# Scatter parts two attention units apart, and joined 512-column second products in the 256-token slots

## The chip, the cores and the metric

The kernel runs on one core of a Trainium2 chip. The metric is the device time of one execution in microseconds (us), as the median of several runs. Engines are called PE (matrix products), PEld (the loading of weights for them), DVE (vector), ACT (activation), POOL (GpSimd) and SP (which only issues DMAs here).

## What is computed

An attention without softmax is followed by a mixture of eight experts, each token going to one expert. All numbers are float32, and the kernel keeps that accuracy by splitting operands in a high and a low part.

```python
# B, S, D = 8, 2496, 256; d_qk = 64; E, F = 8, 1024
scores = matmul(z, z.T) / S
x = u * matmul(maximum(scores, 0) ** 2, v)          # per batch
logits = x @ w_gate
e = argmax(logits); gate = softmax(logits)[e]
eom = sigmoid(x @ w_output_gate)
h = maximum(x @ w1[e], 0)                            # F = 1024
out = gate * eom[e] * (h @ w2[e])
```

## The kernel before

**Attention.** For each of 8 batches there are 5 chunks of queries (the first has 448 columns, the others 512), and for each chunk 10 key pairs. One (batch, chunk, pair) is a unit; there are 400, in the order of the list `units`. A unit has `scores` or `take` (the attention matrix of the pair, made by PE, ACT and DVE two units ahead, `LOOK`) and `weigh` (line 394), its products with v: 10 or 12 matmuls into the two PSUM banks of the chunk.

**The tail of a chunk.** When a chunk is done, a `Tail` (line 414) takes its result through gating, logits, choice of expert and position, and at last a scatter of the token rows to the table `xs` in DRAM. Each unit that follows calls `advance` (line 598) of every living tail once, behind its `weigh`. So a step of the tail falls on one unit, and `TAIL` is the number of the last step that does something; a tail is kept until its step count reaches it. Steps 0 to 9 fall on the ten units of the next chunk, and from step 10 on the tail runs beside its successor. The scatter itself has four parts: `scatter_part` (line 577) issues one small ACT instruction that turns row numbers to integers (`idx`, line 581) and then 3 or 4 indirect DMAs on POOL (line 585), each for 128 segments of token rows. Their data lie in `xr` (line 469), which has two buffers, so a tail's buffer is written again by the transpose of the tail after the next (line 470). SP and POOL run in the order in which the program is written, and so do PE, ACT and DVE.

**Experts.** The tokens of an expert stand together in `xs`, and slots read them: 27 + 3 slots of 512 tokens, 7 of 288 to 480, and 8 of 256 that always run. Ten more of 256 run only under two `tc.If` when the counts of tokens want them. A slot's `up` (line 988) makes one bank of hidden values (two of the eight blocks f in a 256-token slot, four banks in all), `down` (line 1017) the second product of that bank. `run` (line 1266) lets `down` follow three `up`s later (`BEHIND`), and the last slot of a run has its second products in one piece in `whole` (line 1035), first for 128 tokens (part 0), then for the other 128 (part 1).

**The second product of a 256-token slot.** `term` (line 1046) makes for a block f and a part three matmuls of 256 columns: hidden high times weight low, hidden low times weight high, hidden high times weight high, all added into the first 256 columns of a PSUM bank. The hidden values are the stationary operand here and the weights the moving one:

```python
for k, (hx, ww) in enumerate(((hh, 1), (hl, 0), (hh, 0))):
    w = wb[4 + f // 2][:, ww]
    y, st, mv = self.o[part][:, :D], hx[:, at + part * P : ...], w[:, ds_ : ds_ + D]
```

`end_rows` (line 1068) scales the bank by the gate and moves it to `y` with one ACT instruction for each part; `finish` (line 1123) then writes the rows to the output with indirect DMAs on POOL. The wider slots (`columns`, line 1076) use the other orientation and aren't touched.

**Between the two.** The list `later` spreads the last two tails' steps over the first slots (lines 1252 to 1262).

Of the kernel before, what the change touches and what calls it, by code (L numbers as in the profile page):

```python
# [11 lines left out]
AF = mybir.ActivationFunctionType  # L12
ALU = mybir.AluOpType
# [4 lines left out]
P = 128  # L18
B, S, D, DQ = 8, 2496, 256, 64
# [5 lines left out]
T = 256  # L25
# [34 lines left out]

REST = S - (NCH - 1) * CH - 2 * P

TAIL = 15

N_HELD = 2

# [10 lines left out]
def attention_moe(ctx, tc, zt, zq_in, ut, v, wg, w12, out):  # L77
    nc = tc.nc
# [25 lines left out]
        out=sums[0:32].rearrange("p (a m) -> p a m", a=4),  # L104
        in_=ones[0:32].rearrange("p (a m) -> p a m", a=4),
# [308 lines left out]
    class Tail:  # L414
# [183 lines left out]
        def advance(self):  # L598
            k = self.step
            self.step += 1  # L600
            (
                self.gate,
                lambda: (self.split(0), self.split(1)),
                self.rows,
                self.logits,
                self.turn,
                self.choose,
                self.pick,
                self.factor,
                lambda: (self.finish(), self.place()),  # L610
                self.scatter,
                lambda: None,
                lambda: self.scatter_part(0),
                lambda: self.scatter_part(1),
                lambda: self.scatter_part(2),
                lambda: self.scatter_part(3),
                lambda: None,
            )[min(k, TAIL)]()


    def t1(name, shape, dt=F32, tag=None):
        return pool.tile([1] + shape, dt, name=name, tag=tag or name)
# [247 lines left out]
    def pads():  # L870

        pad = pool.tile([P, ROW], F32, name="pad", tag="lt")
        nc.gpsimd.memset(pad, 0.0)
        nc.gpsimd.memset(pad.bitcast(I32)[:, SEG - 1 : SEG], NOTOK)
        ends = t1("ends", [E], I32)
        nc.vector.tensor_copy(out=ends, in_=carry[0][0:1])
        yield
        for e in range(E + 1):
            if e < E:
                at = nc.sync.value_load(ends[0:1, e : e + 1], min_val=e * CAP, max_val=e * CAP + N)  # L880
                seg = xs_rows[bass.ds(at, TW), :]
            else:
                seg = xs_rows[E * CAP : E * CAP + TW, :]
            it = nc.sync.dma_start(
                out=seg.rearrange("(p q) d -> p q d", q=4), in_=pad.unsqueeze(1).to_broadcast([P, 4, ROW])
            )
            tc.add_to_no_dep_group(last_scatters, it.ins)
            yield
# [3 lines left out]
    class Slot:  # L892
# [142 lines left out]
        def whole(self):  # L1035

            self.o = [ps_o.tile([P, CH], F32, name="o") for _ in range(2)]
            self.begin_rows()
            for part in range(2):
                for f in range(8):  # L1040
                    self.term(f, part)
                self.end_rows(part)
            if not self.held:
                self.finish()

        def term(self, f, part):

            wb, n = self.w, self.n
            bank, at = self.hidden(f)
            hh, hl = self.h[bank]  # L1050
            ds_ = (f % 2) * D
            for k, (hx, ww) in enumerate(((hh, 1), (hl, 0), (hh, 0))):
                w = wb[4 + f // 2][:, ww]
                if n == T:
                    y, st, mv = self.o[part][:, :D], hx[:, at + part * P : at + (part + 1) * P], w[:, ds_ : ds_ + D]
                else:
                    y, st, mv = self.o[part][:, :n], w[:, ds_ + part * P : ds_ + (part + 1) * P], hx[:, :n]
                nc.tensor.matmul(  # L1058
                    out=y, lhsT=st, rhs=mv, start=f == 0 and k == 0, stop=f == 7 and k == 2
                )  # L1060
# [4 lines left out]
            else:  # L1065
                self.y = pool.tile([P, 4, D], F32, name="y", tag="xr", bufs=2)

        def end_rows(self, q):
            nc.scalar.activation(
                out=self.y[:, q].rearrange("p (a k s) -> p k a s", a=4, k=2),  # L1070
                in_=self.o[q][:, :D].rearrange("p (k a s) -> p k a s", a=4, k=2),
                func=AF.Copy,
                scale=self.m[:, q, 0:1],
            )

        def columns(self):
            n = self.n
# [102 lines left out]
    def prepare(k):  # L1180
        while to_load and to_load[0][0] - to_load[0][1] <= k:
            to_load.pop(0)[2].load()
        while to_split and to_split[0][0] <= k:
            to_split.pop(0)[2].split()

    attn = {}
    tail = nxt = o = None
    tails = []
# [23 lines left out]
    for k, (b, c, jp) in enumerate(units):  # L1212
# [16 lines left out]
        if b == B - 1:  # L1229
# [4 lines left out]
            at = (c, pos)  # L1234
# [11 lines left out]
        if pos == NPAIR - 1:  # L1246
            tail = nxt
            tails = [it for it in tails if it.step < TAIL] + [tail]
        prepare(k)
# [1 line left out]

    idle = lambda: None
    later = [idle] * (4 * 12)
    for k in (0, 2, 6, 10, 14):
        later[k] = tails[0].advance
    for k in (*range(1, 22, 2), 22, 29, 32, 35):
        later[k] = tail.advance
    more, fill = other_tables(), pads()
    for _ in range(29):
        later += [idle, lambda: next(more, None)]  # L1260
# [73 lines left out]
    with tc.If(used > N_MAIN + 1):  # L1334
        part = slots[last + 1 :]
# [63 lines left out]
```

## Time and profile before

| | us |
|---|---|
| runs: median (lowest, highest) | 2200.44 (2196.61, 2205.82), 3 runs |
| the profiled execution's own time | 2191.03 |
| its span in the trace | 2189.2 |
| PE busy | 2163.7 (99%) |
| PEld busy | 1828.4 (84%) |
| DVE busy | 1752.4 (80%) |
| ACT busy | 1452.0 (66%) |
| POOL busy | 940.2 (43%) |

How to read it: "busy" is the time in which an engine had an instruction in work. Matmuls overlap each other, and the end of one is modelled, so the share of PE says that it hardly ever starved and not how fast it went; that is read from the starts of successive matmuls. The granted PE clock is 0.99 to 1.00 of full speed in all 40 slices of the page. Attention lasts to about 1310 us, the 256-token slots run from about 2090 us to the end.

### The profile page before, as it was taken

How to read it: one execution, taken by the hardware profiler on the slowest of the kernel's cores; microseconds unless marked ns; L12 is line 12 of the kernel's file. 1: busy time of each engine (PE TensorE's matmuls, PEld its weight loads, DVE VectorE, ACT ScalarE, POOL GpSimd, SP SyncE). 2: the span in 40 equal slices, each digit the busy share in tenths (PEclk: the TensorE clock that was granted, in tenths of full speed). 3: DMA queues.
4: the chain of work that ended last, by engine and by line, in shares of the span. 5: the costliest groups of instructions: out<-in, count | busy, mean ns of one | idle time of the engine just before them, and what ended most of it. 6: DMA issues, size and time to landing. Idle time of an engine off the chain costs nothing. (4 is left out here: it accounts for less than half of the span.)

```text
span 2189.2 us, 35155 instructions
## 1 busy us (share of the span) xinstructions
PE 2163.7 (99%) x10207; PEld 1828.4 (84%) x10207; DVE 1752.4 (80%) x2884; ACT 1452.0 (66%) x2494; POOL 940.2 (43%) x829
## 2 busy tenths in 40 slices
PE   9999999999999999999999999999999999999998
PEld 7888788788788788888788888888888898888998
DVE  8898898898898898898898897676666766666676
ACT  8768768768778767767768765555555555555565
POOL 1365565565565564665565574321212111121222
PEclk9999999999999999999999999999999999999999
DMA  6695795794785785784784694535566766666542
GB/s 211 210 240 169 215 242 167 215 241 167 222 235 171 222 232 166 223 234 166 217 239 163 216 266 114 150 95 154 178 188 188 217 210 200 198 187 201 184 148 79
DMA packets 467738, 423.88 MB, mean 194 GB/s; under 512 B 156077, under 2 KB 366638, under 8 KB 467536
## 3 DMA queue, kind: packets, MB, share of 16 engines
q1 hardware_dynamic: 439952, 379.97, 59.3%
q0 software_dynamic: 27584, 41.58, 5.5%
q8 instruction: 82, 1.34, 0.3%
q14 instruction: 120, 0.98, 0.1%
HBM read 292.21 MB, written 158.66 MB: 206 GB/s over the span
## 5 line engine op out<-in xcount | busy, mean ns | idle before, releaser
L585 POOL DMA_INDIRECT xs<-xr,idx x624 | 766.1, 1228 | 597.8 <-ACT idx L581 422.1
L403 PE MATMUL o<-ah,v 128*128 128x512 f32 (+1 forms) x3200 | 845.8, 387 | 9.0 <-ACT ah L277 6.9
L403 PEld LDWEIGHTS o<-ah,v 128*128 128x128 f32 x3200 | 596.1, 188 | 120.7 <-ACT ah L277 10.7
L403 PE MATMUL o<-al,v 128*128 128x512 f32 (+1 forms) x1520 | 463.8, 386 | 0.5
L1012 ACT ACTIVATE hh<-sc 128x512 fp32r<-128x512 f32 (+7 forms) x328 | 190.1, 580 | 391.1 <-PE sc L1003 348.8
L1125 POOL DMA_INDIRECT out<-y,meta x156 | 159.0, 1019 | 629.1 <-ACT y L1115 558.3
L1013 DVE SCALAR_TENSOR_TENSOR hl<-sc,hh 128x512 fp32r<-128x512 f32 (+7 forms) x328 | 218.2, 665 | 262.3 <-ACT hh L1012 248.5
L1003 PE MATMUL sc<-xh,w 128*128 128x512 f32 (+8 forms) x1440 | 399.0, 362 | 1.8 <-issue 1.8
L1058 PE MATMUL o<-hh,w 128*128 128x512 f32 (+7 forms) x1184 | 400.2, 379 | 0.0
L403 PEld LDWEIGHTS o<-al,v 128*128 128x128 f32 x1520 | 283.9, 188 | 58.6 <-DVE al L281 6.6
L281 DVE TENSOR_TENSOR al<-a,ah 128x1024 fp32r<-128x1024 f32 (+1 forms) x199 | 233.1, 1171 | 111.0 <-ACT ah L277 91.0
L1003 PEld LDWEIGHTS sc<-xh,w 128*128 128x128 f32 x1440 | 258.2, 188 | 40.6 <-issue 1.3
L272 ACT ACTIVATE a<-sc 128x512 f32<-128x512 f32 (+1 forms) x398 | 207.6, 572 | 105.9 <-PE sc L271 44.1
L1058 PEld LDWEIGHTS o<-hh,w 128*128 128x128 f32 x1184 | 221.2, 188 | 38.9
L957 DVE TENSOR_TENSOR w<-raw,w 128x512 fp32r<-128x512 f32 x368 | 246.1, 680 | 2.8 <-ACT w L956 2.2
L1058 PE MATMUL o<-hl,w 128*128 128x512 f32 (+7 forms) x592 | 224.5, 379 | 0.0
L956 ACT CAST w<-raw 128x512 fp32r<-128x512 f32 x368 | 220.1, 615 | 0.0
L385 ACT CAST ah<-z 128x1024 fp32r<-128x1024 f32 x192 | 199.5, 1047 | 20.9 <-DMA z<-td 17.3
L275 ACT ACTIVATE a<-a 128x1024 f32<-128x1024 f32 (+1 forms) x199 | 203.6, 1023 | 6.3
L1003 PE MATMUL sc<-xl,w 128*128 128x512 f32 (+8 forms) x720 | 202.3, 362 | 0.0
L389 DVE TENSOR_TENSOR al<-z,ah 128x1024 fp32r<-128x1024 f32 x160 | 194.5, 1216 | 8.3 <-ACT ah L385 3.8
L270 PE MATMUL sc<-z,hl 128*128 128x512 f32 (+1 forms) x398 | 152.8, 384 | 5.0 <-ACT a L272 4.2
(201 smaller groups left out, 2395.5 us busy)
## 6 DMA issues: line engine op xcount, KB each, us to landing
raw<-in_w SPq DMA_DIRECT2D x368, 256.0 KB
z<-td SPq DMA_DIRECT2D x647, 128.0 KB
td<-t SPq DMA_DIRECT2D x160, 512.0 KB
raw<-in_v SPq DMA_DIRECT2D x80, 256.0 KB
u<-in_ut SPq DMA_DIRECT2D x32, 512.0 KB
ym<-yd SPq DMA_DIRECT2D x126, 128.0 KB
sx<-xs SPq DMA_DIRECT2D x120, 128.0 KB
yd<-yt SPq DMA_DIRECT2D x30, 512.0 KB
```

The lines of the kernel that those rows point to most:

```text
L272: nc.scalar.activation(out=a[:, q, :w], in_=sc[:, :w], func=AF.Relu)
L275: nc.scalar.activation(out=a[:, :, :w], in_=a[:, :, :w], func=AF.Square)
L281: nc.vector.tensor_tensor(out=al[:, :, :w], in0=a[:, :, :w], in1=ah[:, :, :w].bitcast(F32), op=ALU.subtract)
L385: nc.scalar.copy(out=ah, in_=z)
L389: nc.vector.tensor_tensor(out=al, in0=z, in1=ah.bitcast(F32), op=ALU.subtract)
L403: nc.tensor.matmul(out=o[d][:, :w], lhsT=vv[:, q, d * P : (d + 1) * P], rhs=rhs, start=begins and q == 0 and k == 0, stop=ends and q == 1 ...
L585: it = nc.gpsimd.indirect_dma_start(out=xs[:, :], out_offset=bass.IndirectOffsetOnAxis(ap=idx[:, n - first : n - first + 1], axis=0), in_= ...
L956: nc.scalar.copy(out=ww[:, 0], in_=wr)
L957: nc.vector.tensor_tensor(out=ww[:, 1], in0=wr, in1=ww[:, 0].bitcast(F32), op=ALU.subtract)
L1003: nc.tensor.matmul(out=hp[:, at : at + n], lhsT=wb[2 * d + f // 4][:, ww, fs], rhs=xx[:, d, :], start=k == 0, stop=k == 5,)
L1013: nc.vector.scalar_tensor_tensor(out=lo, in0=hp[:, 0:used], scalar=0.0, in1=ho.bitcast(F32), op0=ALU.max, op1=ALU.subtract)
L1058: nc.tensor.matmul(out=y, lhsT=st, rhs=mv, start=f == 0 and k == 0, stop=f == 7 and k == 2)
```

## The change

Two separate edits. The first moves parts 1, 2 and 3 of a chunk's scatter from steps 12, 13 and 14 of the tail to 13, 15 and 17, with empty steps between, and so `TAIL` from 15 to 18. The two tails that are still living when attention ends call `scatter_part` by name from the list `later`, at the positions that they had. The second edit, in the 256-token slots, makes of three matmuls two: hidden high times the pair (weight high, weight low) as one product of 512 columns into both halves of a PSUM bank, and hidden low times weight high into the first half. `end_rows` then adds the second half, scaled, to `y` with two DVE instructions for each part. Only part 1 of `whole` keeps the three matmuls and the single ACT instruction (`narrow`).

```diff
-TAIL = 15
+TAIL = 18
...
                 self.scatter,
                 lambda: None,
                 lambda: self.scatter_part(0),
+                lambda: None,
                 lambda: self.scatter_part(1),
+                lambda: None,
                 lambda: self.scatter_part(2),
+                lambda: None,
                 lambda: self.scatter_part(3),
                 lambda: None,
             )[min(k, TAIL)]()
...
             for part in range(2):
                 for f in range(8):
-                    self.term(f, part)
-                self.end_rows(part)
+                    self.term(f, part, part == 1)
+                self.end_rows(part, part == 1)
             if not self.held:
                 self.finish()
 
-        def term(self, f, part):
+        def term(self, f, part, narrow=False):
 
             wb, n = self.w, self.n
             bank, at = self.hidden(f)
             hh, hl = self.h[bank]
             ds_ = (f % 2) * D
+            if n == T and not narrow:
+                y = self.o[part].rearrange("p (k d) -> p k d", k=2)
+                w = wb[4 + f // 2][:, :, ds_ : ds_ + D]
+                hh, hl = [x[:, at + part * P : at + (part + 1) * P] for x in (hh, hl)]
+                nc.tensor.matmul(out=y, lhsT=hh, rhs=w, start=f == 0, stop=False)
+                nc.tensor.matmul(out=y[:, 0], lhsT=hl, rhs=w[:, 0], start=False, stop=f == 7)
+                return
...
-        def end_rows(self, q):
-            nc.scalar.activation(
-                out=self.y[:, q].rearrange("p (a k s) -> p k a s", a=4, k=2),
-                in_=self.o[q][:, :D].rearrange("p (k a s) -> p k a s", a=4, k=2),
-                func=AF.Copy,
-                scale=self.m[:, q, 0:1],
-            )
+        def end_rows(self, q, narrow=False):
+            y = self.y[:, q].rearrange("p (a k s) -> p k a s", a=4, k=2)
+            of = [
+                self.o[q][:, i * D : (i + 1) * D].rearrange("p (k a s) -> p k a s", a=4, k=2) for i in range(2)
+            ]
+            nc.scalar.activation(out=y, in_=of[0], func=AF.Copy, scale=self.m[:, q, 0:1])
+            if not narrow:
+                for k in range(2):
+                    nc.vector.scalar_tensor_tensor(
+                        out=y[:, k], in0=of[1][:, k], scalar=self.m[:, q, 0:1], in1=y[:, k], op0=ALU.mult, op1=ALU.add
+                    )
...
-    for k in (0, 2, 6, 10, 14):
-        later[k] = tails[0].advance
-    for k in (*range(1, 22, 2), 22, 29, 32, 35):
+    for k in range(1, 22, 2):
         later[k] = tail.advance
+    for part in range(4):
+        later[2 + 4 * part] = lambda part=part: tails[0].scatter_part(part)
+        later[(22, 29, 32, 35)[part]] = lambda part=part: tail.scatter_part(part)
```

Three places show how instructions move. The first is PE in a 256-token slot, one `up` and the `down` behind it; `sc` are the first products, `o` the second ones, `hh` and `hl` the hidden high and low parts. Before:

```order
L1003 MATMUL sc<-xh,w 128x256 x2
L1058 MATMUL o<-w,hh 128x256
L1058 MATMUL o<-w,hl 128x256
L1058 MATMUL o<-w,hh 128x256 x2
L1058 MATMUL o<-w,hl 128x256
L1058 MATMUL o<-w,hh 128x256 x2
L1058 MATMUL o<-w,hl 128x256
L1058 MATMUL o<-w,hh 128x256 x2
L1058 MATMUL o<-w,hl 128x256
L1058 MATMUL o<-w,hh 128x256
```

And with the change, the same stretch:

```order
L1006 MATMUL sc<-xh,w 128x256 x2
L1059 MATMUL o<-w,hh 128x512
L1060 MATMUL o<-w,hl 128x256
L1059 MATMUL o<-w,hh 128x512
L1060 MATMUL o<-w,hl 128x256
L1059 MATMUL o<-w,hh 128x512
L1060 MATMUL o<-w,hl 128x256
L1059 MATMUL o<-w,hh 128x512
L1060 MATMUL o<-w,hl 128x256
```

Twelve matmuls of 256 columns became four of 512 and four of 256: the same number of columns in eight instructions.

The second place is DVE in the same slots, behind the split of the next slot's input (`xl`); `w` are splits of weights, `hl` the low part of hidden values, `y` the new instructions. With the change:

```order
L980 TENSOR_TENSOR xl<-xf,xh 128x2x256
L960 TENSOR_TENSOR w<-raw_15258,w 128x512
L1086 SCALAR_TENSOR_TENSOR y<-o,meta,y 128x4x32 x4
L960 TENSOR_TENSOR w<-raw_15297,w 128x512
L960 TENSOR_TENSOR w<-raw_15328,w 128x512
L1016 SCALAR_TENSOR_TENSOR hl<-sc,hh 128x512
```

The four `y` are new; all others stand there in the same order before.

The third place is ACT in attention, in the units in which one tail scatters (`idx`) while the next is at its exponentials (`ex`, `eo`) and its count of places (`both`). Before:

```order
L581 ACTIVATE idx<-row 128x4
L443 CAST xh<-u 128x512 x2
L385 CAST ah<-z 128x1024
L581 ACTIVATE idx<-row 128x4
L385 CAST ah<-z 128x1024
L581 ACTIVATE idx<-row 128x4
L197 CAST v<-raw 128x512
L385 CAST ah<-z 128x1024
L581 ACTIVATE idx<-row 128x4
...
L490 ACTIVATE ex<-dl 128x128
...
L531 COPY both<-hot_101 64x136
```

And with the change:

```order
L581 ACTIVATE idx<-row 128x4
L443 CAST xh<-u 128x512 x2
L385 CAST ah<-z 128x1024 x2
L581 ACTIVATE idx<-row 128x4
L197 CAST v<-raw 128x512
L385 CAST ah<-z 128x1024
...
L581 ACTIVATE idx<-row 128x4
...
L490 ACTIVATE ex<-dl 128x128
L197 CAST v<-raw 128x512
L385 CAST ah<-z 128x1024
L581 ACTIVATE idx<-row 128x4
L531 COPY both<-hot_101 64x136
```

The first `idx` stays, the second moves by one unit, the third by two and the last by three, to just ahead of the next tail's `both`. The order of POOL's own instructions is the same in both kernels.

## Rows read from the trace of the kernel before

**Rows 1.** The page, busy time of each engine over the span.

```profile
PE 2163.7 (99%) x10207; PEld 1828.4 (84%) x10207; DVE 1752.4 (80%) x2884; ACT 1452.0 (66%) x2494; POOL 940.2 (43%) x829
```

**Rows 2.** Groups of PE's instructions: count | busy us, mean ns | idle before, by releaser.

```profile
L403 PE MATMUL o<-ah,v 128*128 128x512 f32 (+1 forms) x3200 | 845.8, 387 | 9.0 <-ACT ah L277 6.9 <-DVE v L198 1.7 <-DVE ah L241 0.2
...
L1003 PE MATMUL sc<-xh,w 128*128 128x512 f32 (+8 forms) x1440 | 399.0, 362 | 1.8 <-issue 1.8
...
L270 PE MATMUL sc<-z,hl 128*128 128x512 f32 (+1 forms) x398 | 152.8, 384 | 5.0 <-ACT a L272 4.2 <-issue 0.7
...
L1058 PE MATMUL o<-w,hh 128*128 128x256 f32 x256 | 50.8, 283 | 0.0
...
L556 PE MATMUL mp<-both,sums 128*128 128x136 bf16 x40 | 9.3, 233 | 0.8 <-ACT both L531 0.8
```

**Rows 3.** PE in order of time, attention with 512 columns: start, us, what.

```profile
599.70 1.07 PE L403 MATMUL o<-ah,v 128*128 128x512 f32 x4
...
603.78 0.39 PE L270 MATMUL sc<-z,hl 128*128 128x512 f32 x1
```

**Rows 4.** PE in order of time, a 256-token slot, two neighbouring `up`s.

```profile
2145.93 0.40 PE L1003 MATMUL sc<-xh,w 128*128 128x256 f32 x2
...
2148.81 0.40 PE L1003 MATMUL sc<-xh,w 128*128 128x256 f32 x2
```

**Rows 5.** A 256-token slot's window: PE, PEld, DVE, ACT, POOL busy; clock, DMA share, GB/s.

```profile
2132.10:2143.60 11.50, 11.50 (x98) 11.50 (x97) 8.74 (x15) 7.62 (x16) 2.44 (x3) 1.00 0.58 173
```

**Rows 6.** Groups by shape, 2000 to 2190 us.

```profile
L1013 DVE SCALAR_TENSOR_TENSOR hl<-sc,hh 128x512 fp32r<-128x512 f32 x42 | 28.9, 688 | 30.1 <-ACT hh L1012 29.8 <-issue 0.2
L1058 PEld LDWEIGHTS o<-w,hh 128*128 128x128 f32 x256 | 42.0, 192 | 0.0
...
L1013 DVE SCALAR_TENSOR_TENSOR hl<-sc,hh 128x416 fp32r<-128x416 f32 x8 | 4.7, 587 | 6.5 <-ACT hh L1012 6.5
```

**Rows 7.** All engines in order of time, the end of the program.

```profile
2179.29 0.47 ACT L1069 ACTIVATE y<-o,meta_h 128x256 f32<-128x256 f32 x1 [0.88 <-issue]
...
2182.16 0.28 PE L1058 MATMUL o<-w,hh 128*128 128x256 f32 x1
2182.48 0.47 ACT L1069 ACTIVATE y<-o,meta_h 128x256 f32<-128x256 f32 x1 [2.72 <-PE o L1058]
2183.22 0.97 POOL L1125 DMA_INDIRECT out<-y,meta_h  x1 [2.22 <-ACTq L1334]
```

**Rows 8.** ACT in order of time, one chunk: first and last `idx`, then `both`.

```profile
702.34 0.20 ACT L581 ACTIVATE idx<-row 128x4 int32<-128x4 f32 x1
...
711.99 0.20 ACT L581 ACTIVATE idx<-row 128x4 int32<-128x4 f32 x1
...
724.08 0.30 ACT L531 COPY both<-hot 64x136 bf16<-64x136 bf16 x1 [1.05 <-DVE cand L492]
```

**Rows 9.** POOL in order of time, that chunk's first and last of 16 indirect DMAs.

```profile
702.81 0.97 POOL L585 DMA_INDIRECT xs<-xr,idx  x1 [12.04 <-ACT idx L581]
...
725.66 1.67 POOL L585 DMA_INDIRECT xs<-xr,idx  x1 [0.30 <-issue]
```

**Rows 10.** DVE in order of time, the transpose that writes that chunk's buffer anew.

```profile
745.71 1.21 DVE L470 STREAM_TRANSPOSE xr<-u 128x1024 f32<-128x1024 f32 x1
```

**Rows 11.** DVE's L281 by shape while POOL scatters (700:725), then while idle (727:736).

```profile
L281 DVE TENSOR_TENSOR al<-a,ah 128x1024 fp32r<-128x1024 f32 x6 | 7.3, 1218 | 0.5 <-ACT ah L277 0.5
...
L281 DVE TENSOR_TENSOR al<-a,ah 128x1024 fp32r<-128x1024 f32 x1 | 1.2, 1226 | 4.8 <-ACT ah L277 4.8
```

**Rows 12.** PE and ACT in order of time, four places in attention.

```profile
731.51 1.21 PE L403 MATMUL o<-ah,v 128*128 128x512 f32 x4 [0.95 <-ACT ah L277]
...
854.90 0.98 ACT L272 ACTIVATE a<-sc 128x448 f32<-128x448 f32 x2 [3.81 <-remote]
855.49 0.50 PE L270 MATMUL sc<-z,hl 128*128 128x512 f32 x1 [3.30 <-ACT a L272]
...
1026.38 1.20 PE L403 MATMUL o<-ah,v 128*128 128x512 f32 x4 [1.62 <-ACT ah L277]
```

## The prediction

> **What bounds the kernel now.** I read the page's busy line first, then the groups of PE's instructions with their idle time, then PE in order of time in the two places that the change touches, then the window of one 256-token slot. The busy line shows PE at work for 2163.7 of 2189.2 us [rows 1]; it loses 25.5 us in all. About 7 us of these lie behind the last matmul (2182.16 us [rows 7]). The groups name most of the rest: L403 waits 6.9 us for ACT's `ah`, L270 4.2 for ACT's `a` and 0.7 for its own issue, L556 0.8 for `both`, L1003 1.8 for its issue in the expert stage [rows 2]. So whatever is done on other engines can give back at most these: 6.9 + 4.2 + 0.7 + 0.8 = 12.6 us in attention. Everything beyond has to come out of PE's own pace.
>
> That pace is read from starts. In attention eighteen matmuls of 512 columns start between 599.70 and 603.78 us [rows 3]: 4.08 / 18 = 0.2267 us each. In a 256-token slot 24 of 256 columns start between 2145.93 and 2148.81 [rows 4]: 2.88 / 24 = 0.120 us each. Two of these cost 0.240 us, one of 512 columns 0.2267: a fixed 13.3 ns for each matmul beside its columns.
>
> **The second edit: fewer, wider products.** Columns stay the same, 768 for a block and part; a triple becomes a pair, so one fixed part is saved. The eight 256-token slots that run have 256 + 128 = 384 second products before (the first number is the group's count [rows 2], and there is one product with hidden low for two with hidden high), that is 128 triples. Eight stay triples (part 1 of the last slot). 120 x 13.3 ns = **1.6 us saved**, and all of it on the path, as PE has no gap in these slots (11.50 of 11.50 us [rows 5]).
>
> The price is 30 additions on DVE (two for a part, 15 parts). No row shows one of 128 elements from PSUM. Nearest is the like instruction at L1013, 688 ns with 512 elements and 587 with 416 [rows 6]: 1.05 ns an element, so some 285 ns with 128. Bounds: not below the 134 ns that 128 elements cost by the slope alone, not above the 688 of 512. I take 285, as shape and kind are the same. A slot gets four: 1.1 us on top of DVE's 8.74 of 11.5 us [rows 5], 86% instead of 76%. They stand behind ACT's `y` and ahead of two weight splits and one `hl`, so that `hl` comes about 1 us later; its product is three banks of 2.9 us behind, and the next `up` into its PSUM bank too. Cover is some 8 us, the cost on the path nothing. Even at 688 ns a slot would hold 8.74 + 2.75 = 11.49 us of DVE against PE's new 11.52 - 16 x 0.0133 = 11.31: 0.18 us for each of seven slots, **1.3 us lost at worst**.
>
> At the end part 0's additions follow the ACT instruction at 2179.29, three microseconds ahead of the last matmul; part 1 has its old form, so what follows 2182.16 is unchanged [rows 7].
>
> The Trainium skill would price an addition a little lower: its page "VectorE: DVE Perf Modes", in the section on the TRN2 errata, has 120 cycles plus one an element for a PSUM source, by which it is an estimate of 258 ns; the sum stays.
>
> **The first edit: the scatter.** Nothing is added: four `idx` of 0.2 us on ACT and 16 indirect DMAs on POOL for each chunk, as before. The four `idx` now end at 702.34 and 711.99 us in the chunk that I read [rows 8], but POOL works off its queue from 702.81 until 727.33 [rows 9], about 24.5 us or 1.5 us each. A unit has 12 to 16 matmuls, so parts two units apart are 5.4 to 7.3 us apart by PE's pace [rows 3], just about POOL's own 6.1 us for a part. The scatter gets three small pauses and ends perhaps 3 us later: the last `idx` will be just ahead of `both`, 724.08 [rows 8], and four DMAs behind it end at about 730. What is late next? The buffer is written again at 745.71 [rows 10], so 15 us remain for the data to leave it. Bound for that time, from the nearest row: behind the program's last indirect DMA (2183.22 + 0.97) 5.0 us pass to the end of the span [rows 7]. Enough. ACT's last `idx` falls in front of a wait of 1.05 us that ACT has anyway [rows 8]. The other two move between instructions of the same engine and cost it what they cost before. DVE doesn't feel POOL: 1218 ns while POOL scatters, 1226 while it doesn't [rows 11]. The part at the start of the expert stage stays where it was. So I cost this edit at **nothing**; bounds are a gain of at most the 12.6 us above, and a loss that the third rival prices.
>
> **The sum.** 0 - 1.6 = -1.6 us. The profiled execution took 2191.03 us (1.8 beside its span) and would take 2189.4. The median of the runs shown is 9.4 us above it and they spread over 9.2 us, so the runs lose more than this trace shows, where I can't see. I put the difference on the median: 2200.4 - 1.6 = **2198.8 us**. A measurement of this kernel can tell about 0.5%, 11 us, from no change; this is under 0.1%.
>
> **Rivals.**
>
> *The pauses give PE its losses back.* Attention's losses are of two kinds. One comes back at the same place of a batch, five times with up to 0.95 us, as at 731.51. The other stands where a batch starts, with ACT idle for no reason inside the program: ACT waits 3.81 us "remote" at 854.90 and PE then 3.30, and 1.62 at 1026.38 [rows 12]. POOL scatters densely there. The second kind is 12.6 - 5 x 0.95 = 7.9 us. If pauses in the DMA traffic end it, the time is 2200.4 - 1.6 - 7.9 = 2190.9; if the first kind goes too, 2186.2. Against it: the same traffic passes, in 27 us instead of 24.5, and the two places hold 4.9 of the 7.9, so the other batch starts lost little under as dense a scatter.
>
> *Loads of weights set the pace.* PEld is busy for all 11.50 us of the window [rows 5], and one load lasts 192 ns [rows 6]. If each load stood in the way, 120 fewer would give 120 x 0.192 = 23 us: 2177. Against it: matmuls start every 120 ns [rows 4], less than one load, so loads must overlap.
> The Trainium skill holds that rule: the page "TensorE: Matmul & The Clock Gate", section "The mechanism" of its part on packing small matmuls, says that a load overlaps with matmuls under way only when it goes to another row group. By it the sum would be -23 us; the rows on the pace of 256 columns speak against it.
>
> *The longer scatter lengthens the gaps where a batch starts* (the other side). It now reaches 3 us further, into the fetches for the next units. ACT's gap of 3.81 us cost PE 3.30 [rows 12]: some 0.5 us are covered there, and from there on PE pays all of it. If all seven batch starts lost 3.3 us, PE would lose 23.1 instead of 7.9: 15.2 - 1.6 = 13.6 us more, 2214.0. For it: these gaps differ from batch to batch with nothing in the program to explain it. Against it: POOL's work per microsecond falls.
>
> *The pair does not save what it says.* The 512-column product reads its moving operand in two pieces and writes both halves of a bank; rows 3 show the pace for one piece. If the joint costs 13 ns, nothing is left: 2200.4.
>
> **How the numbers follow.** The forecast has 0.70; gaps given back at batch starts 0.12, all losses in attention given back 0.05; loads 0.02; longer gaps 0.05; no saving 0.06. Faster by over 0.5% (below 2189.4) are 0.05 + 0.02 = 0.07, slower by over 0.5% is 0.05, within it 0.88. For the range I take the runs' own spread around the forecast, 2195.0 to 2204.2, extend it down to the first rival (2190.9), up by the 1.3 us of DVE and some of the longer gaps: 2190 to 2207.
>
> **What would show it.** In the 256-token slots the distance of two `up`s should fall from 2.88 to 2.88 - 4 x 0.0133 = 2.83 us, and the slot from 11.5 to 11.3; DVE there 9.6 to 9.9 us; each addition near 285 ns. PE's fixed part would be refuted by a distance that stays 2.88. In attention POOL's 16 DMAs should stand in four groups with short pauses, and the waits of L403 and L270 at 6.9 and 4.2 us, give or take two or three. Wrong would be the whole if these fell to nothing or passed 20 us together.

## The result

| | before | changed kernel |
|---|---|---|
| median of the runs (us) | 2201.99 (4 runs, 2196.61 to 2205.82) | 2174.38 (4 runs, 2166.37 to 2176.09) |
| ratio, 95% interval | | 0.9884 [0.9863, 0.9906] |
| profiled execution, its span | 2191.03, 2189.2 | 2173.87, 2172.1 |

The forecast was 2198.8 us with a range of 2190 to 2207. The change took off 1.2%, some 26 us, and the time lies far below the range. The two traces differ by less, 17.1 us; the traces tell where those went, and the rest of the difference of the medians is in runs without a trace.

The page of the changed kernel, its busy line, and the groups of PE that answer to [rows 1, 2]:

```profile
PE 2155.7 (99%) x10087; PEld 1823.6 (84%) x10087; DVE 1761.7 (81%) x2914; ACT 1452.4 (67%) x2494; POOL 934.4 (43%) x829
```
```profile
L403 PE MATMUL o<-ah,v 128*128 128x512 f32 (+1 forms) x3200 | 844.3, 386 | 3.1 <-DVE v L198 1.7 <-issue 1.1 <-DVE ah L241 0.2
...
L1006 PE MATMUL sc<-xh,w 128*128 128x512 f32 (+8 forms) x1440 | 399.4, 362 | 2.2 <-DVE hl L1016 2.0 <-issue 0.2
...
L270 PE MATMUL sc<-z,hl 128*128 128x512 f32 (+1 forms) x398 | 152.2, 382 | 0.7 <-ACT a L272 0.7
...
L1059 PE MATMUL o<-w,hh 128*128 128x512 f32 x120 | 43.8, 398 | 0.0
```

L403 no longer waits for ACT's `ah` (6.9 us before) and L270 for `a` only 0.7 us instead of 4.2: what the prediction named as the sign that it would be wrong. Of the 120 pairs L1059 is one half.

Where the time went is told by one matmul for each chunk, L556. Its first and its 36th, before and (second fence) with the change, PE in order of time:

```profile
75.01 0.23 PE L556 MATMUL mp<-both,sums 128*128 128x136 bf16 x1
...
1220.76 0.23 PE L556 MATMUL mp<-both,sums 128*128 128x136 bf16 x1
```
```profile
74.43 0.23 PE L556 MATMUL mp<-both,sums 128*128 128x136 bf16 x1
...
1197.74 0.23 PE L556 MATMUL mp<-both,sums 128*128 128x136 bf16 x1
```

The seven batches between take 1145.75 us before and 1123.31 now, **22.4 us less**. Now each batch takes 160.5 us (distances of L556: 32.9, 31.0, 29.2, 33.1, 34.3 in every one); before, a batch took 161.5 to 167.3. Ahead of them 0.6 us are gained; behind them the end of attention gives 4.1 us back (the first expert product starts at 1297.1 instead of 1316.1: 19.0 us), and from there to the end of the span it is 875.0 us instead of 873.2. So the gain is all in attention.

PE's idle rows in attention had summed to 12 us, so they understate the loss. PE in order of time, the place of [rows 12] at 731.51 with the unit around it, and the same unit now:

```profile
729.49 0.39 PE L270 MATMUL sc<-z,hl 128*128 128x512 f32 x1
...
737.44 0.39 PE L270 MATMUL sc<-z,hl 128*128 128x512 f32 x1
```
```profile
719.17 0.39 PE L270 MATMUL sc<-z,hl 128*128 128x512 f32 x1
720.08 1.07 PE L403 MATMUL o<-ah,v 128*128 128x512 f32 x4
...
725.52 0.39 PE L270 MATMUL sc<-z,hl 128*128 128x512 f32 x1
```

The unit took 7.95 us and takes 6.35: 1.60 us for a stall shown as 0.95. A row's idle counts from the modelled end of a matmul, 0.39 us behind its start, where the next start is due after 0.23; and the matmuls behind the stall start more slowly (the first four last 1.21 us together [rows 12], now 1.07). After the longest stall (855.49, 3.30 us) the granted clock fell as well. Windows of PE before; columns: PE busy (count), granted clock, DMA share, GB/s:

```profile
853.00:856.00 3.00, 0.51 (x2) 1.00 0.53 185
856.00:859.60 3.60, 3.60 (x11) 0.53 0.00 0
859.60:862.00 2.40, 2.40 (x14) 1.00 0.43 176
```

PE, idle for 3.30 us before, then ran for some 3.4 us at 1.2 GHz instead of 2.4 and started 11 matmuls where 16 or more were due. So not all slices of the kernel before have a granted clock of 0.99 to 1.00: this one (821 to 876 us) has 0.97, the last one 0.98.

### The profile page after: what moved, and what is told of

The parts are those of the page before. It is cut to its first block, busy times and chain, and to the rows that moved or that the text cites. A ratio compares the mean times of both kernels' runs of the same rounds, so it can differ in the third digit from the quotient of the medians.

```text
span 2172.1 us, 34947 instructions
## 1 busy us (share of the span) xinstructions
PE 2155.7 (99%) x10087; PEld 1823.6 (84%) x10087; DVE 1761.7 (81%) x2914; ACT 1452.4 (67%) x2494; POOL 934.4 (43%) x829
## 5 line engine op out<-in xcount | busy, mean ns | idle before, releaser
L585 POOL DMA_INDIRECT xs<-xr,idx x624 | 753.9, 1208 | 592.5 <-ACT idx L581 384.0
L403 PE MATMUL o<-ah,v 128*128 128x512 f32 (+1 forms) x3200 | 844.3, 386 | 3.1 <-DVE v L198 1.7
L403 PEld LDWEIGHTS o<-ah,v 128*128 128x128 f32 x3200 | 596.4, 188 | 110.4 <-DVE v L198 2.4
L403 PE MATMUL o<-al,v 128*128 128x512 f32 (+1 forms) x1520 | 462.1, 385 | 0.7 <-issue 0.7
L1139 POOL DMA_INDIRECT out<-y,meta x156 | 163.6, 1049 | 625.2 <-ACT y L1129 557.8
L403 PEld LDWEIGHTS o<-al,v 128*128 128x128 f32 x1520 | 285.7, 188 | 54.2 <-issue 1.6
L281 DVE TENSOR_TENSOR al<-a,ah 128x1024 fp32r<-128x1024 f32 (+1 forms) x199 | 233.5, 1173 | 85.1 <-ACT ah L277 44.9
L385 ACT CAST ah<-z 128x1024 fp32r<-128x1024 f32 x192 | 198.7, 1047 | 24.8 <-DMA z<-td 19.8
L389 DVE TENSOR_TENSOR al<-z,ah 128x1024 fp32r<-128x1024 f32 x160 | 194.8, 1217 | 12.3 <-issue 6.1
L277 ACT CAST ah<-a 128x1024 fp32r<-128x1024 f32 (+1 forms) x150 | 151.9, 1013 | 4.8
```

What stands on the lines that cost most here:

```text
L281: nc.vector.tensor_tensor(out=al[:, :, :w], in0=a[:, :, :w], in1=ah[:, :, :w].bitcast(F32), op=ALU.subtract)
L385: nc.scalar.copy(out=ah, in_=z)
L389: nc.vector.tensor_tensor(out=al, in0=z, in1=ah.bitcast(F32), op=ALU.subtract)
L403: nc.tensor.matmul(out=o[d][:, :w], lhsT=vv[:, q, d * P : (d + 1) * P], rhs=rhs, start=begins and q == 0 and k == 0, stop=ends and q == 1 ...
L585: it = nc.gpsimd.indirect_dma_start(out=xs[:, :], out_offset=bass.IndirectOffsetOnAxis(ap=idx[:, n - first : n - first + 1], axis=0), in_= ...
```

## The experiments

**What was measured.** I call a start of ACT late when ACT had been idle for over 0.25 us and began at least 1.4 us after the start of the product whose completion it waited for by the program's counts (the median is 0.43 us); starts that also wait for a fetch (L385) are left out. The window is 75 to 1250 us. The kernel before has 19 such starts, 2.7 to 6.4 us behind the start of the product (one 1.6), with ACT idle for 0.4 to 3.8 us just before; the changed kernel has none. In all 19 the product starts inside a row of POOL's indirect DMAs without a pause, 8 us or more behind the row's beginning. "Remote" in a line means that the profile names no instruction that ended the wait.

**A long row is not enough.** The kernel before has 28 rows of 15 or 16 DMAs without a pause in the window, four in each batch. Of the 14 that belong to the fourth and fifth chunks of a batch 12 hold late starts, of the 14 of the second and third chunks one does, although ACT, idle, took a product 19 times there as deep in the row (8 us or more). The pattern is the same in e2, f1, f3 and k2. And the changed kernel doesn't have its pauses everywhere. In each batch it keeps one row of 12 DMAs and one of 16 (25.7 us), and in the rows of 16 ACT is on time. POOL, PE and ACT of the changed kernel:

```profile
466.70 1.01 POOL L585 DMA_INDIRECT xs<-xr,idx  x1 [4.66 <-ACT idx L581]
468.02 0.97 POOL L585 DMA_INDIRECT xs<-xr,idx  x1 [0.30 <-issue]
...
491.09 1.34 POOL L585 DMA_INDIRECT xs<-xr,idx  x1 [0.32 <-issue]
```
```profile
479.04 0.28 PE L377 MATMUL sc<-z,hl 128*128 128x256 f32 x1
```
```profile
479.35 0.66 ACT L378 ACTIVATE z<-sc 128x256 f32<-128x256 f32 x2 [2.00 <-PE sc L377]
```

ACT starts 0.31 us behind PE, 12.3 us into the row; in seven batches 14 such starts, 12 and 26 us into these rows, are all on time. So a long row without a pause doesn't by itself make ACT late; what else the rows of the fourth and fifth chunks meet, no run shows.

Theories at the start: A, unbroken rows of scatter DMAs on POOL delay PE's completions, and pauses cure that; B, it is the place of `idx` on ACT; C, it is the second edit. The results (before beside them on the same chip):

| run | us | ratio, interval | before there | late starts |
|---|---|---|---|---|
| e1_scatter_alone | 2174.93 | 0.9881 [0.9855, 0.9907] | 2201.1 | 0 |
| e2_pairs_alone | 2199.2 | 0.9992 [0.9973, 1.0011] | 2201.1 | 25 |
| e3_pool_pauses | 2197.0 | 0.9981 [0.9963, 1.0000] | 2201.1 | 2 |
| e4_late_run | 2190.7 | 0.9950 [0.9931, 0.9969] | 2201.1 | 0 |
| e5_dense_plus1 | 2166.07 | 1.0001 [0.9991, 1.0010] | 2166.15 | 0 |
| e6_dense_plus3 | 2168.41 | 1.0014 [1.0005, 1.0024] | 2166.15 | 0 |
| e7_two_columns | 2166.03, one run | | 2166.15 | 0 |
| f1_before_again | 2194.5 | 0.9998 [0.9983, 1.0012] | 2195.91 | 23 |
| f2_change_again | 2177.28 | 0.9916 [0.9903, 0.9929] | 2195.91 | 0 |
| f3_pairs_again | 2195.46 | 0.9996 [0.9982, 1.0011] | 2195.91 | 20 |
| g1_dense_plus1 | 2166.33 | 1.0001 [0.9992, 1.0011] | 2166.32 | 0 |
| g2_dense_plus3 | 2171.47 | 1.0020 [1.0011, 1.0030] | 2166.32 | 0 |
| g3_two_columns | 2167.03, one run | | 2166.32 | 0 |
| g4_last_dense | 2166.42 | 1.0001 [0.9991, 1.0010] | 2166.32 | 0 |
| h1_dense_plus3 | 2168.3 | 1.0017 [1.0008, 1.0027] | 2165.91 | 0 |
| h2_two_columns | 2166.39, one run | | 2165.91 | 0 |
| k1_change_third | 2178.66 | 0.9922 [0.9903, 0.9941] | 2195.86 | 0 |
| k2_two_columns | 2196.76, one run | | 2195.86 | 25 |

The letters e1 to e4, e5 to e7, f, g, h and k are six chips. **They are of two kinds:** on three (and in the first comparison) the kernel before takes 2196 to 2202 us, on three 2166. I call them the first and the second kind. Each chip was met once, so it isn't shown that the kind belongs to a chip for good.

**e1 and e2: each edit alone.** e1 has the diff's first part (`TAIL = 18`, empty steps, `later`), e2 its second (`term`, `end_rows`, `whole`).

> Only the first edit: parts at steps 11, 13, 15, 17, second products as before. Theory A (the pauses between scatter parts let PE's completions reach ACT in time) and theory B (it is the place of the four idx among ACT's instructions, not POOL's pauses): attention ends near 1297 us instead of 1316, PE's idle in attention falls from about 12 us to under 3, and the time is within 4 us of the changed kernel's 2174. Theory C (the gain comes from the second edit or from its side effects): the stalls stay and the time is about 2200.

> Only the second edit: 512-column second products, parts of the scatter one step apart as before. Theories A and B: attention as before (end near 1316 us, about 12 us of PE idle), the 256-token slots at most 2 us shorter, time 2198 to 2202. Theory C: time near 2178.

The first edit alone gives the whole gain and leaves no late start, so theory C is out; the second has no effect that these runs can tell.

**e3: pauses made in another way.** The kernel before, with

```diff
+PAUSE = 12
...
+            if part and not (self.b == B - 1 and self.c == NCH - 1):
+                for _ in range(PAUSE):
+                    nc.gpsimd.memset(rest_of_pool, 0.0)
```

the last three lines at the head of `scatter_part`.

> The kernel before, idx at its old places on ACT (steps 11 to 14), with twelve small memsets on POOL (about 2 us) ahead of parts 1, 2 and 3, so that POOL's DMAs stand in four groups with pauses. Theory A: the stalls go as in the changed kernel, end of attention 1297 to 1302 us, time 2175 to 2183. Theory B: stalls of 10 us and more stay, end of attention 1313 or later, time 2196 to 2206.

By its time, and by the first expert product at 1321.6 us, this looked like theory B, but the trace says otherwise: 2 late starts instead of 19, and batches of 160.5 us among others of 161 to 168. Rows broken without any move of `idx` lost nearly all their late starts, so B is out. The memsets also put POOL's DMAs later, so the run doesn't tell the pauses from the new places of the DMAs. What was lost instead is another wait. DVE, then PE in order of time (lines stand 3 lower in this kernel):

```profile
647.57 1.25 DVE L473 STREAM_TRANSPOSE xr<-u 128x1024 f32<-128x1024 f32 x1 [6.32 <-DMA xs<-xr,idx]
```
```profile
649.98 1.22 PE L405 MATMUL o<-al,v 128*128 128x512 f32 x2 [4.24 <-DVE al L391]
```

The pauses were too long: POOL fell behind, the transpose into `xr` waited 6.32 us for the scatter that still read it, and PE 4.24 behind DVE. Waits of this kind, for `al` from DVE, are 12.7 of the 13.8 us that PE idles in the window.

**e4: a control that changed nothing where it should.** All DMAs of a chunk written behind its last `idx`:

```diff
+            self.ready = getattr(self, "ready", []) + [
+                (n, idx[:, n - first : n - first + 1]) for n in range(first, end)
+            ]
+            if part < 3 and not self.split_late:
+                return
```

> The changed kernel with idx at its new places on ACT (steps 11, 13, 15, 17), but all 13 to 16 indirect DMAs of a chunk issued behind the last idx, in one unbroken run of about 24 us. Theory A: the stalls come back, PE idle in attention 8 to 15 us, end of attention 1310 to 1320 us, time 2190 to 2205. Theory B: no stalls, time 2172 to 2179.

POOL didn't go by the place in the program: it still took each DMA as soon as that part's `idx` was there, in the same groups as in the changed kernel (for one chunk from 337.71, 345.30, 351.62 and 359.27 us, with waits of 2.40, 0.67 and 2.07 between). So the run says nothing for or against unbroken rows; that its time falls into theory A's range is chance. Its loss against e1 (16 us by the medians, 9 by the spans) lies behind 1250 us, since its batches take 160.5 us; I didn't follow it.

**e5 to e7, g1 to g4, h1, h2: where nothing was to be found.** Four parts one unit apart but one or three units later (`TAIL` and empty steps ahead of part 0), and the scatter cut to two columns:

```diff
-                    out=xs[:, :],
+                    out=xs_two[:, :],
...
-                in_=self.xr[:, n, :],
+                in_=self.xr[:, n, SEG - 2 : SEG],
```

> The kernel before with its four parts still one unit apart, but all one unit later (steps 12 to 15). Theory P (what matters is which other work the unbroken scatter meets, so its place in the chunk, not its pauses): the stalls shift or shrink but don't vanish, PE idle in attention between 40 and 1260 us is 3 to 12 us, time 2182 to 2200. Theory L (an unbroken run of 16 DMAs is enough to delay PE's completions): as before, 10 to 15 us idle, 2196 to 2205.

> The same, three units later (steps 14 to 17, so that the last part stands where the changed kernel has it). Theory P: no or nearly no stalls (under 2 us of idle before 1260 us), attention ends at 1292 to 1302 us, time 2172 to 2188. Theory L: stalls of 10 to 15 us at other places, 2196 to 2205.

> The kernel before with the same number of indirect DMAs and segments, but only the last two of a segment's 66 columns scattered (the experts read their tokens from u instead, so their results mean nothing and only attention is compared). Theory D (the scatter's bytes on the DMA queues delay completions): ACT's late starts behind PE vanish, PE idle in attention falls from 12 us to under 3, first expert product near 1297 us. Theory Q (POOL's own work on the indirect DMAs does it, whatever the bytes): late starts of 2.8 us and more stay, idle 10 to 15 us, first expert product at 1312 or later.

All three met a chip where the kernel before takes 2166 us and nothing is late, so neither theory was tried. I ran them again, with a fourth that puts back the parts' old distance for two tails of the last batch:

```diff
+            if self.b == B - 1 and self.c in (1, 2) and k > 10:
+                if k < 15:
+                    self.scatter_part(k - 11)
+                return
```

> The kernel before with its four parts one unit apart and all one unit later (steps 12 to 15), again, to be run where the kernel before takes about 2200 us. Theory P (the place in the chunk): fewer late starts of ACT behind PE than before, or at other places, 2180 to 2196. Theory L is already spoken against by the late unbroken run; it would give 2196 to 2205. Where before takes 2166 us: the same as before, and nothing learnt.

> All parts three units later (steps 14 to 17), again. Theory P: no late starts between 100 and 1260 us, batches of 160.5 us, time 2172 to 2190 where before takes 2200. Theory L: 15 late starts or more, 2196 to 2205.

> The kernel before with all its indirect DMAs, but two of 66 columns scattered (experts read u in place of their tokens, so only attention is compared), again. Theory D (bytes on the queues): no late starts, first expert product near 1293 us. Theory Q (POOL's own work, whatever the bytes): 15 late starts or more, first expert product at 1310 to 1320, where before has these.

> The changed kernel with the parts of chunks 1 and 2 of the last batch one unit apart, as before, so that POOL is free earlier for the last two chunks. If the loss of the changed kernel around 1298 us (chunk 39 takes 35 us instead of 31, and the expert stage 2 to 4 us more) comes from POOL's late queue there: 4 to 7 us less than the changed kernel on the same kind of chip, so 2167 to 2173 where before takes 2200. Otherwise 2174 to 2178.

> All four parts three units later, one unit apart, once more. Where before takes about 2200 us: theory P (place) none or few late starts, 2172 to 2190; theory L (length) 15 or more, 2196 to 2205. Where before takes 2166 us: 2168 to 2172 as the two times before.

> Two of 66 columns scattered (experts read u in place of their tokens), once more. Where before takes about 2200 us: theory D (bytes) no late starts, first expert product near 1293 us; theory Q (POOL's work on the indirect DMAs) 15 or more, first expert product at 1310 to 1320. Where before takes 2166 us: 2166 to 2167, no late starts.

Both were chips of the second kind again. (What g1's text says against theory L counts e4 as an unbroken run, which it wasn't.) They do show two things. g4, the changed kernel but for two tails, is worth nothing there: 1.0001 [0.9991, 1.0010]. And the scatter put off by three units costs 2 to 5 us, by the wait that e3 has. DVE in e6, near the end of attention:

```profile
1278.54 1.25 DVE L470 STREAM_TRANSPOSE xr<-u 128x1024 f32<-128x1024 f32 x1 [3.72 <-DMA xs<-xr,idx]
```

**f1 to f3: the three kernels again, on another chip.**

> The kernel before, unchanged, for a trace of it on the chip of this comparison. Theory R (ACT's late starts behind PE arise on the chip of the first comparisons and not on the one where this kernel took 2166 us): where it takes about 2166 us the trace has no late start of ACT behind PE, chunks repeat every 160.5 us per batch, and attention ends near 1293 us; where it takes about 2200 us there are 15 or more late starts. Theory P (the place of the scatter decides on any chip): 15 or more late starts in either case.

> The changed kernel, unchanged. Theory R: on a chip where the kernel before takes about 2166 us the change is worth only what it does itself: the second edit's 0 to 4 us, 2162 to 2170, so a ratio of 0.998 to 1.002; on a chip where before takes 2200 us, 2172 to 2178 again. Theory P: faster by 1% on either chip.

> The second edit alone. Theory R and the sum of the prediction: 1.6 us less than the kernel before on any chip, so 2164.5 where before takes 2166 us (ratio 0.9993, told apart from 1 only where the runs spread little); 2199 where before takes 2200.

The chip was of the first kind, and the first comparison came back: 23 late starts at the same places of the batches in f1, 20 in f3, none in f2. One of them, in f1: PE, then ACT, then POOL in order of time.

```profile
356.65 0.59 PE L366 MATMUL sc<-z,hl 128*128 128x192 f32 x4
```
```profile
359.46 0.33 ACT L367 ACTIVATE z<-sc 128x192 f32<-128x192 f32 x1 [2.72 <-remote]
360.19 0.33 ACT L367 ACTIVATE z<-sc 128x192 f32<-128x192 f32 x1 [0.39 <-PE sc L271]
```
```profile
342.44 0.97 POOL L585 DMA_INDIRECT xs<-xr,idx  x1 [5.84 <-ACT idx L581]
343.72 0.98 POOL L585 DMA_INDIRECT xs<-xr,idx  x1 [0.30 <-issue]
...
359.93 1.22 POOL L585 DMA_INDIRECT xs<-xr,idx  x1 [0.30 <-issue]
```

The four products are over by 357.24; ACT, idle, takes the first result at 359.46, 2.8 us after the products' start. That is 17 us deep in a row of DMAs without a pause. The same place in the changed kernel of the first comparison:

```profile
352.01 0.58 PE L366 MATMUL sc<-z,hl 128*128 128x192 f32 x4
```
```profile
352.41 0.55 ACT L367 ACTIVATE z<-sc 128x192 f32<-128x192 f32 x2 [0.47 <-PE sc L366]
```
```profile
345.39 0.97 POOL L585 DMA_INDIRECT xs<-xr,idx  x1 [2.41 <-ACT idx L581]
...
351.71 0.97 POOL L585 DMA_INDIRECT xs<-xr,idx  x1 [0.66 <-ACT idx L581]
...
359.37 1.05 POOL L585 DMA_INDIRECT xs<-xr,idx  x1 [2.07 <-ACT both L531]
```

ACT follows PE by 0.40 us, and POOL's row has its pauses of 2.41, 0.66 and 2.07 us.

**k1 and k2: once more on a chip of the first kind.**

> The changed kernel, unchanged. Theory R (the gain is the late starts of ACT, which only some chips have): where the kernel before takes about 2166 us, 2164 to 2170, ratio 0.999 to 1.002; where it takes about 2200 us, 2172 to 2178, ratio 0.988 to 0.992.

> Two of 66 columns scattered (experts read u in place of their tokens), a last time. Where before takes about 2200 us: theory D (bytes) no late starts, first expert product near 1293 us; theory Q (POOL's work) 15 or more, first expert product at 1310 to 1320. Where before takes 2166 us: 2166 to 2167.

k1 lies just outside what was expected of it (2178.66 us, ratio 0.9922). k2 settles the bytes: theory D is out. Scattering 2 of 66 columns leaves all 16 DMAs on POOL and takes 97% of the scattered data away, and the late starts stay, 25 of them. As the DMAs and their segments stay as many, this doesn't tell POOL's own work from the number of segments on the queues. The same kernel, at the same place, on the two kinds of chip: PE, then ACT in k2 (lines stand 1 lower):

```profile
523.16 0.58 PE L367 MATMUL sc<-z,hl 128*128 128x192 f32 x4
```
```profile
525.97 0.33 ACT L368 ACTIVATE z<-sc 128x192 f32<-128x192 f32 x1 [2.69 <-remote]
```

and in h2:

```profile
512.80 0.59 PE L367 MATMUL sc<-z,hl 128*128 128x192 f32 x4
```
```profile
513.20 0.55 ACT L368 ACTIVATE z<-sc 128x192 f32<-128x192 f32 x2 [0.56 <-PE sc L367]
```

2.81 us against 0.40. POOL's first DMA lies 14.2 us ahead of the product in both (508.95 and 498.58). So in the same kernel, at the same place of the same unbroken row, ACT is late on one chip and on time on the other.

**Left open.** Of theory A it is shown that breaking up the rows takes the late starts away, not that any long row makes them. Open are: why ACT is late behind PE in those rows, and why only on some chips; whether it is the pauses that help or the new places of the DMAs (the rows put off by one or three units, unbroken, never met a chip of the first kind); whether the changed kernel itself gains anything on a chip of the second kind, where only g4 ran; and whether g4 wins back the end. There the changed kernel loses 5 to 7 us on chips of the first kind (spans of 2169.5 to 2172.1 against g4's 2164.8 on the other kind), part of it by a late start again. ACT, then PE, in the changed kernel of the first comparison:

```profile
1301.49 0.60 ACT L1015 ACTIVATE hh<-sc 128x512 fp32r<-128x512 f32 x1 [8.82 <-PE sc L1006]
```
```profile
1302.86 0.50 PE L1006 MATMUL sc<-xh,w 128*128 128x512 f32 x1 [1.49 <-DVE hl L1016]
```

The product that ACT takes here began its last matmul at 1298.27 us. DVE was late behind PE at this place too:

```profile
1297.00 0.17 DVE L563 TENSOR_TENSOR carry<-mp,carry 128x8 f32<-128x8 f32 x1 [1.78 <-PE o L403]
```

Its `mp` is L556's at 1294.28 us, 2.72 us earlier; in the kernel before DVE takes that chunk's `mp` 0.85 us behind. This speaks for PE's word being late and not ACT. One of the 19 late starts says the same. PE, then ACT in the kernel before:

```profile
723.23 0.39 PE L271 MATMUL sc<-z,hl 128*128 128x512 f32 x1
```
```profile
725.30 0.22 ACT L535 ACTIVATE eo<-osel 128x16 f32<-128x16 f32 x1 [0.91 <-DVE osel L526]
728.20 1.09 ACT L272 ACTIVATE a<-sc 128x512 f32<-128x512 f32 x2 [2.68 <-PE mp L556]
```

At 725.30 ACT starts under 0.1 us behind DVE's `osel`; the product that began on PE at 723.23 it takes only at 728.20.

So no version was shown to beat both kernels on both kinds of chip.

## Why the prediction was wrong

**The step that failed is the first edit's cost of nothing.** It was argued from what the edit adds (nothing), from DVE not feeling POOL [rows 11], and from POOL keeping up. The first two hold, and the third but for the end of attention, where 4.1 us are given back. What was missing is that ACT feels POOL: by e1 and e3 it starts late behind PE in some unbroken rows of DMAs, and no longer once these rows are broken up. The prediction foresaw the three small pauses and gave them no gain in its sum; with e1 at 0.9881 they, or the new places of the DMAs that come with them, are the whole effect. The wait at 731.51 [rows 12] came behind such a late start and the one at 854.90 is one; they were read as waits without a cause in the program. The four groups of DMAs that were forecast stand only for the fourth chunk of a batch; the fifth has three groups, and the third chunk's DMAs have no pause at all.

**The bound of 12.6 us was the second error.** It was taken from idle rows [rows 2], and idle rows are not what a stall costs: 0.95 shown were 1.60 lost, and a stall of 3.30 brought 3.4 us at half the clock behind it. The trace of before held the better bound: its shortest distance of L556 for each chunk sums to 160.5 us a batch, which is 22.5 us under what the seven batches took. Against that bound the rival would have stood at 2176.

**The first rival was right in kind and refused for the wrong reason.** Breaking up the rows did give PE its losses back, of both kinds. I gave all of it 0.05 because the same traffic passes in nearly the same time; k2 shows that the bytes were never the point. Its price was too small by the same error as the bound: 14.2 us at most (12.6 + 1.6) against 26.

**The longer scatter** did not lengthen the gaps at batch starts: they are gone (e1: no idle row of PE over 0.15 us between 40 us and the first expert product). The point that the rival rested on, gaps that differ from batch to batch, was one of the late starts.

**The second edit was right in sign, smaller than forecast, and too small to be timed.** The changed kernel's neighbouring `up`s, to set beside [rows 4]:

```profile
2130.92 0.40 PE L1006 MATMUL sc<-xh,w 128*128 128x256 f32 x2
...
2133.78 0.40 PE L1006 MATMUL sc<-xh,w 128*128 128x256 f32 x2
```

The distances alternate between 2.85 and 2.86, 2.855 on average, instead of 2.88: 0.025 us for four pairs, 6 ns each where 13.3 were put down. 120 x 6 ns is 0.75 us, not 1.6. So the pace gives about half of what was put down, between the forecast and the rival that saw no saving; that it is the joint of the 512-column product that takes the rest is not shown. The traces' whole stage of 256-token slots, from its first product to PE's last, says 0.3 to 1.2: 97.6 to 97.8 us without the pairs (before, e1, e3, f1) and 96.3 to 96.6 with them (the changed kernel, e2, f2, f3, k1), on the second kind of chip 95.75 (g1) and 95.45 (g4). e2 and f3 (0.9992 and 0.9996, both intervals hold 1) can't tell 0.75 from 1.6.

**DVE.** The additions, and the window of a slot to set beside [rows 5]:

```profile
L1086 DVE SCALAR_TENSOR_TENSOR y<-o,meta,y 128x128 f32<-128x128 f32 x20 | 5.6, 345 | 0.0
```
```profile
2121.00:2132.50 11.50, 11.50 (x82) 10.76 (x82) 9.62 (x18) 7.65 (x15) 3.29 (x2) 1.00 0.63 181
```

345 ns each, not 285, still within the bounds (134 to 688); DVE at 9.62 us of the window is inside the forecast 9.6 to 9.9 (as in two of three neighbouring windows; the earliest has 10.94), and PE has no gap. The Trainium skill's page "VectorE: DVE Perf Modes", section on the TRN2 errata, had led to an estimate of 258 ns; the trace has 345, and the measurement decides.

**Weight loads** don't set the pace: with 120 fewer, PEld is down from 11.50 to 10.76 us of a window and the slot is shorter by 0.1 us, not by 16 times 0.19. The Trainium skill's page "TensorE: Matmul & The Clock Gate", section "The mechanism", in its sentence on row groups, would have had the time fall by 23 us from this edit alone (the section also names a background weight buffer, to which a load may go ahead); it fell by about that much, but e1 and e2 show that it was the other edit. A total that agrees with a rule isn't evidence for the rule.

**The range.** Its lower end was the small form of the first rival; no case reached below the 2177 of the weight loads. The median of before and its profiled execution differed by 9.4 us, which was named as a loss that the trace doesn't show; a second look at the batches' lengths (161.5 to 167.3) would have told that the loss varies and so isn't PE's own pace.

## What to carry to other kernels

Measure what stalls cost by the repeating work itself: take the shortest time of each piece that repeats, sum it, and compare with the whole, since idle rows gave 12 us where 22 were lost. Where a consumer starts late although its producer had long finished, look at what a third engine does in that time; here ACT was late in some rows of 15 or 16 indirect DMAs on POOL, and breaking up these rows, with waits of 0.7 to 2.4 us, ended it. Look also at the like rows where nothing is late: they show that the row alone isn't the cause. Time such a change on more than one chip: it was worth 0.8 to 1.2% on the chips that have the late starts, and nearly the same kernel (g4) nothing, within 0.1%, on one that hasn't.

## What was not expected of the hardware

The same kernel takes 2166 us on three chips and 2196 to 2202 us on three others, and in traces of one kernel on either kind (k2 and h2) the difference can be read: 25 late starts against none, in identical instructions. PE's own semaphore updates, in the trace's records, stand in bursts on the chips of the first kind, several within 0.3 us (six at 728.1 us of the kernel before, 4.9 us behind the 723.2 us at which the product that ACT waited for began), mostly 15 us or more behind the start of one of POOL's rows; on the other chips no more than two stand together, about once a chunk. But the bursts don't show when an update reached ACT. On the first kind about 30% of the records are missing in the window (739 of PE's updates for 1035 products that make one in the kernel before, 694 for 1051 in the changed one), and at 720.64 us of the kernel before ACT starts on products that end at 720.18 and 720.42, with no update of PE on record between 717.24 and 728.11. The changed kernel still has such a burst in every batch (at 302.53 us, for one) and no late start. An edit that takes no work away in attention thus gained 26 us where the kernel before takes 2200 us, and nearly the same edit nothing where it takes 2166.
